# Lightning attention and a mixture of depths: the twelfth 128-token group as one wide chunk, and the expert's first pieces among the products of that step

## The chip, the cores and the metric

The kernel runs on one core of a Trainium2 chip. A core has five engines that run side by side, each with its own instruction queue: TensorE (PE; its weight loads are shown apart as PEld), VectorE (DVE), ScalarE (ACT), GpSimd (POOL) and SyncE (SP). SP only issues DMA transfers here, ACT and POOL issue some as well, and 16 DMA engines carry all of them. The time is the device time of one execution, in microseconds (us); less is better.

## The reference

There are two parts, all in float32. The first is a linear attention with decay, for 4 batches, 8 heads, 768 tokens and head size 64. In words, for each head with its decay `lam`:

```python
intra = (q_b @ k_b.T * Dmask) @ v_b          # Dmask[i,j] = lam**(i-j) for i >= j, else 0
inter = (q_b * lam**(pos+1)) @ kv_state      # what the earlier blocks left
out_b = intra + inter
kv_state = lam**block * kv_state + (k_b * lam**(block-1-pos)).T @ v_b
```

The reference cuts the tokens into blocks of 64. The result doesn't depend on the block length, apart from rounding, as long as the powers follow it.

The second part takes the attention's output `x`, the 8 heads side by side (512 values a token). A score `x @ w_gate` is made for each token. In each batch the 128 tokens with the highest scores go through an expert, and the others stay as they are:

```python
h = maximum(x[top] @ w1, 0)                  # 512 -> 1024
out[top] = x[top] + sigmoid(score[top]) * (h @ w2)   # 1024 -> 512
```

## The kernel before

**Groups and steps.** The 3072 tokens are 24 groups of 128 (`NG`), six to a batch (`NT`). Group `g` is rows `128*(g % 6)` of batch `g // 6`. One loop (L704) runs `g` from -1 to 23; one pass is called a step here. The order of all instructions is written out by hand (`manual_schedule`, L64), and each engine works through its own in that order. An instruction that waits therefore holds up everything behind it on its engine.

**Wide and narrow.** A group is either one chunk of 128 tokens ("wide") or two chunks of 64 ("narrow"). `wide(g)` at L192 decides by `WIDE`, which is 11: groups 0 to 10 are wide, 11 to 23 narrow. The batch ends lie at groups 5, 11, 17 and 23. The pieces of a group, each a function:

- `transposes(g, "qT" or "kT")` (L207): four TensorE transposes of the group's queries or keys into one PSUM bank, and an ACT copy to SBUF (L222).
- `queries_decayed(g)` (L224): POOL multiplies qT by powers of `lam` (L229 wide, L231 narrow) into `qs`. `keys_decayed(g)` (L195): the same for the keys, into `kd` (L200).
- `scores(g)` (L238): products of keys and queries into the PSUM tile `su`. Wide: 8 products of 64 by 128 (L249). Narrow: 16 of 64 by 64 (L255), into the first 256 columns of each half.
- `masked(g)` (L260): DVE multiplies the scores by the decay mask into `p`, 128x1024 when wide (L269), 128x512 when narrow (L275).
- `state_products(g)` (L281): `kd` times values. Wide: into a bank of its own (L293), and nothing for the last group of a batch, whose state nobody needs. Narrow: into the last 256 columns of `su` (L302); for the last group of a batch only the first chunk, since the second needs that state.
- `decay_state(n)` (L308, POOL L315) and `next_state(n)` (L320, DVE L332 and L334): the state of chunk `n` is the decayed old one plus the products.
- `from_states(g)` (L337: L344 wide, L355 narrow) and `from_scores(g)` (L363: L371 wide, L378 narrow): 16 products each into the PSUM tile `o`, the second on top of the first.
- `settle(g)` (L385): in narrow steps a small ACT copy that waits for the first of these sums. `outputs(g)` (L393): ACT copies `o` to `x_b`, one copy when wide (L400), three when narrow (L406, L408).
- `gate_scores(g)` (L418): DVE makes the tokens' scores, from `o` when wide (L422), from `x_b` when narrow (L429).

A float32 product shows as two matmul records and two weight-load records in the profile, so 16 products are "x32".

**Ranking and experts.** `row`, `compare`, `column_sums` (L439 to L493) count for each token how many tokens of its batch have a higher score; `find`, `tokens`, `fetch` pick the top 128 and gather their rows from the output in HBM. `expert(b, i)` (L546) returns 17 pieces for one batch: one `gate` (four transposes, L554, and an ACT copy, L559), eight `hidden` (L590, a Relu on ACT at L594) and eight `back` (L602). `products(n)` (L669) runs the next `n` of these pieces; its calls are strewn among the attention's products. `finish` (L610) runs at the next `flush()` after the last piece: a DVE operation (L615) and an indirect store on the POOL queue (L620).

**Banks.** Four PSUM banks `m` are handed out in turn by `bank()` (L176), the one used longest ago first. While an expert is in its `back` pieces one of them is held. A product into a bank waits until the last reader of that bank is done.

**A wide step** `g` (L714 to L802) does, in this order: the row and the comparison of group `g-1`, column sums, the transposes of group `g+1`, `queries_decayed(g+1)`, `from_scores(g)`, `outputs(g)`, `store(g)`, `gate_scores(g)`; then `state_products(g+1)`, `scores(g+1)`, `from_states(g+1)`, `keys_decayed(g+2)`, `next_state`, `decay_state`, and `masked(g+1)`. The last wide step, 10, differs because group 11 is narrow: it runs `scores(11)`, `masked(11)` and already the transposes of group 12 ahead of `state_products(11)`, and leaves `from_states(11)` to the next step.

**A narrow step** `g` (L803 to L850) does: `scores(g+1)`, `from_states(g)`, `settle(g)`, `load_v(g+2)`, `state_products(g+1)`, the first state, `masked(g+1)`, `from_scores(g)`, `outputs(g)`, `keys_decayed(g+2)`, a piece of the expert, column sums and the row of `g-1`, the transposes of `g+2`, the store, the second state, a `flush`, a piece, the comparison of `g-1`, `gate_scores(g)`, a piece, a `flush`. Where a batch ended six groups ago (steps 11 and 17) it begins with the expert's pieces and runs the first one ahead of all else (L804 to L807). So step 11 runs four pieces of batch 0's expert, and steps 12 to 15 three each.

**Loads.** SP issues keys and queries three groups ahead (L705), then parts of the expert's weights and the stores of batch 1; keys and queries have three buffers each, values six. The values of groups 2 to 13 are issued by ACT (`load_v`, L87): in wide steps from 4 on at the top of the step (L708), in narrow ones behind `settle` (L812).

Of the kernel before, what the change touches and what calls it, by code (L numbers as in the profile page):

```python
# [17 lines left out]
def kernel(  # L18
# [20 lines left out]
    NT = S // L  # L39
# [3 lines left out]
    NGR = (CAP + 127) // 128  # L43
    NG = B * NT
# [4 lines left out]
    SOON = 3  # L49
    SECOND = range(2, NT * 2 + 2)  # L50
    WEIGHTS = {9: 1, 10: 2, 11: 1, 12: 3, 13: 3, 14: 2}
    WIDE = 11
    FIRST_V = 4
    WARM = 8
    TINY = 2.0 ** -125
# [31 lines left out]
    def load_v(g):  # L87
        if g not in SECOND:
            return
        b, c = divmod(g, NT)  # L90
        nc.scalar.dma_start(
            out=loaded[g][2][:],
            in_=v[b, :, c * L : (c + 1) * L, :].rearrange("h p d -> p h d"),
        )
# [81 lines left out]
    def bank(hold=False):  # L176
        t = next(t for t in free if not any(t is x for x in held))
        free[:] = [x for x in free if x is not t] + [t]
        if hold:
            held.append(t)  # L180
        return t
# [5 lines left out]
    def quarters():  # L187
        for hp in range(NHP):
            for hh, c in ((0, 0), (1, 1), (1, 0), (0, 1)):
                yield hp, hh, c  # L190

    def wide(g):  # L192
        return g < WIDE

# [12 lines left out]
    def transposes(g, name, part=None):  # L207
        if g >= NG:
            return
        t = loaded[g][1 if name == "qT" else 0]  # L210
        dsts = qTs if name == "qT" else kTs
        hps = range(NHP) if part is None else range(part * NHP // 2, (part + 1) * NHP // 2)
        if not part:
            banks_[name] = bank()
            dsts[g] = att.tile([128, NHP, L], FP32, name=name)
        tp = banks_[name]
        for hp in hps:
            nc.tensor.transpose(  # L218
                tp[:, hp * L : (hp + 1) * L], in_=t[:, 2 * hp : 2 * hp + 2, :], identity=ident[:]
            )  # L220
        at = slice(hps[0] * L, (hps[-1] + 1) * L)
        nc.scalar.copy(out=dsts[g][:].rearrange("p a i -> p (a i)")[:, at], in_=tp[:, at])  # L222
# [15 lines left out]
    def scores(g, part=None):  # L238
        if g >= NG:
            return  # L240
        hps = range(NHP) if part is None else range(part * NHP // 2, (part + 1) * NHP // 2)
        qT, kT = qTs[g], kTs[g]
        if part != 0:
            qTs.pop(g), kTs.pop(g)
        if wide(g):
            to = o_ if part == 1 else su
            for hp in hps:
                for hh in range(2):
                    nc.tensor.matmul(  # L249
                        to[:, hh, hp * L : (hp + 1) * L], lhsT=kT[half[hh], hp, :],  # L250
                        rhs=qT[half[hh], hp, :], start=True, stop=True, skip_group_check=True,
                    )
            return
        for hp, hh, c in quarters():
            nc.tensor.matmul(  # L255
                su[half[c], hh, hp * C : (hp + 1) * C], lhsT=kT[half[hh], hp, half[c]],
                rhs=qT[half[hh], hp, half[c]], start=True, stop=True, skip_group_check=True,
            )

    def masked(g, part=None):  # L260
        if g >= NG:
            return
        if wide(g):
            if not part:
                ps_[g] = att.tile([128, 2, NHP * L], FP32, name="p", bufs=2)
            at = slice(0, NHP * L) if part is None else slice(
                part * NHP * L // 2, (part + 1) * NHP * L // 2
            )
            nc.vector.tensor_tensor(  # L269
                out=ps_[g][:, :, at], in0=(o_ if part == 1 else su)[:, :, at],  # L270
                in1=mask_w[:].rearrange("p a b i -> p a (b i)")[:, :, at], op=ALU.mult,
            )
            return
        p = att.tile([128, 2, NHP * L], FP32, name="p", bufs=2)
        nc.vector.tensor_tensor(  # L275
            out=p[:, :, : NHP * C], in0=su[:, :, : NHP * C],
            in1=mask[:].rearrange("p a b i -> p a (b i)"), op=ALU.mult,
        )
        ps_[g] = p

    def state_products(g):  # L281
        if g >= NG:
            return
        vn, kd = loaded[g][2], kds.pop(g)
        if wide(g):
            if g % NT == NT - 1:
                return
            ub = bank()
            us[g] = ub
            for hp in range(NHP):  # L290
                for hh in range(2):
                    h = 2 * hp + hh
                    nc.tensor.matmul(  # L293
                        ub[half[hh], hp * D : (hp + 1) * D], lhsT=kd[:, h, :], rhs=vn[:, h, :],
                        start=True, stop=True, skip_group_check=True,
                    )
            return
        for hp, hh, c in quarters():
            if c == 1 and g % NT == NT - 1:
                continue  # L300
            h = 2 * hp + hh
            nc.tensor.matmul(  # L302
                su[half[hh], c, NHP * C + hp * D : NHP * C + (hp + 1) * D],
                lhsT=kd[half[c], h, :], rhs=vn[half[c], h, :],
                start=True, stop=True, skip_group_check=True,
            )
# [202 lines left out]
    def tokens(b, i):  # L509
        e = hits_.pop((b, i))  # L510
        pk = bank()[:, :2]
        for t in range(NT):
            nc.tensor.matmul(
                pk, lhsT=e[:, t, :], rhs=place[:, b * NT + t, :],
                start=(t == 0), stop=(t == NT - 1),
            )
        two = mod.tile([128, 2], FP32, name="two")
        nc.vector.tensor_copy(two[:], pk)
        tok = const.tile([128, 1], I32, name=f"tok{b}_{i}")
        nc.vector.scalar_tensor_tensor(  # L520
            out=tok[:], in0=two[:, 0:1], scalar=128.0, in1=two[:, 1:2],
            op0=ALU.mult, op1=ALU.add,
        )
        toks[b, i] = tok
# [14 lines left out]
    def fetch(b, i):  # L539
        xs = mod.tile([128, HD], FP32, name="xs")  # L540
        nc.gpsimd.indirect_dma_start(
            out=xs[:], out_offset=None, in_=rows_upto(b), in_offset=rows_at(b, i),
        )
        xss[b, i] = xs
# [122 lines left out]
    pieces = []  # L667

    def products(n):  # L669
        for _ in range(min(n, len(pieces))):  # L670
            pieces.pop(0)()
# [15 lines left out]
    def ends(g):  # L687
        return g >= 0 and g % NT == NT - 1
# [15 lines left out]
    for g in range(-1, NG):  # L704
        loads_to(g + ahead(g), g)  # L705
        if g == 0:
            load_v(2)
        if FIRST_V <= g < WIDE:  # L708
            load_v(g + 2)
# [4 lines left out]
        if wide(g):  # L714
# [42 lines left out]
            if NGR and ends(g - 3):  # L757
                for i in range(NGR):
                    tokens((g - 3) // NT, i)
            if not wide(g + 1):  # L760
                scores(g + 1)
                masked(g + 1)
                for name in ("qT", "kT"):
                    transposes(g + 2, name)
            if g != 1:
                state_products(g + 1)
            if g > 0 and wide(g + 1):
                scores(g + 1)
            if wide(g + 1):
# [14 lines left out]
            if NGR and ends(g - 3):  # L784
                for i in range(NGR):
                    fetch((g - 3) // NT, i)
            if g > 1 and wide(g + 1):
                masked(g + 1)
            if g == 1:
                nc.scalar.copy(  # L790
# [10 lines left out]
                column_sums(g - 2)  # L801
                find((g - 2) // NT)  # L802
        else:  # L803
            if ends(g - 6) and g + 1 < NG:  # L804
                for i in range(NGR):
                    pieces.extend(expert((g - 6) // NT, i))
                products(1)  # L807
# [99 lines left out]
```

## Time and profile before

| | us |
|---|---|
| median of 3 runs (lowest, highest) | 173.01 (171.4, 173.9) |
| the profiled execution | 172.47 |
| its span, first to last instruction | 170.7 |
| PE busy | 160.3 (94%) |
| DVE busy | 107.0 (63%) |
| POOL busy | 86.8 (51%) |
| ACT busy | 71.0 (42%) |
| DMA: moved in the span | 32.20 MB |

The page's first part gives busy time and share of each engine. A second part cuts the span into 40 equal slices, one digit each, the busy share in tenths; PEclk is the clock granted to TensorE and DMA the mean share of the 16 DMA engines. The chain is the work that ended last, followed back from the last instruction: each step goes to what released it, or to the instruction before it on its engine. "issue" in it is time in which an engine waited for nothing that the profile shows. In a timeline a row is: start and duration in us, engine, line, operation, tiles written and read, shape, number of instructions, and in brackets how long the engine stood idle before and what ended that. Durations of single matmuls overlap, as TensorE is pipelined; the chain's pieces do not.

### The profile page before, as it was taken

The numbers are of one execution on the slowest core, as the hardware profiler recorded it, in microseconds if no ns is written. First come the engines' busy times: TensorE is split into PE (matmuls) and PEld (weight loads), VectorE is DVE, ScalarE is ACT, GpSimd is POOL, SyncE is SP. The second block draws the span as 40 slices with busy tenths as digits, with TensorE's granted clock in tenths as the row PEclk, the third lists the DMA queues.
The fourth block names the chain that finished last, engine by engine and source line by source line (L and its number), as shares of the span: only waits on it lengthen the run. The fifth ranks groups of instructions, "written<-read, shape, count | busy, mean of one in ns | idle before, by whom it ended". The sixth has DMA issues, their size and how long they took to land.

```text
span 170.7 us, 7463 instructions
## 1 busy us (share of the span) xinstructions
PE 160.3 (94%) x3228; PEld 134.1 (79%) x3228; DVE 107.0 (63%) x289; ACT 71.0 (42%) x188; POOL 86.8 (51%) x96
## 2 busy tenths in 40 slices
PE   7999999899899888999999999999999999999990
PEld 7788798788789767999767689998677698469970
DVE  1862569859986544685897996568879745340010
ACT  3355338434344344475346356635633553023100
POOL 1387864517759634485586659648767200201022
PEclk9999999999999999999999999999999999999998
DMA  4999999999999999999999988877024450111000
GB/s 107 223 222 214 238 198 268 279 276 296 236 262 277 284 314 218 349 213 317 256 220 205 246 211 177 187 217 217 28 103 139 161 198 3 20 45 61 0 31 31
DMA packets 82608, 32.20 MB, mean 189 GB/s; under 512 B 75792, under 2 KB 77840, under 8 KB 82576
## 3 DMA queue, kind: packets, MB, share of 16 engines
q1 hardware_dynamic: 66560, 21.50, 56.9%
q10 hardware_dynamic: 15360, 8.13, 18.6%
q0 software_dynamic: 656, 2.10, 3.8%
q8 instruction: 25, 0.41, 1.1%
q14 instruction: 7, 0.06, 0.1%
HBM read 24.38 MB, written 7.34 MB: 186 GB/s over the span
## 4 chain that ended last, share of the span: by engine, by line
PE 70%; DVE 7%; issue 6%; DMA 5%; POOL 5%; SPq 4%; ACT 1%; POOLq 1%; DVEq 0%
PE m L590 18%; PE m L602 13%; PE m L218 9%; PE su L255 4%; PE o L378 4%; PE o L371 4%; SPq L82 4%; DMA qn<-in_q_dram 4%; PE su L302 4%; PE su L249 3%; PE o L355 3%; POOL qs L229 2%; PE o L344 2%; PE m L449 2%; POOL kd L200 2%
## 5 line engine op out<-in xcount | busy, mean ns | idle before, releaser
L590 PE MATMUL m<-xsT,w_sb 128*128 128x128 f32 x256 | 32.3, 279 | 0.1
L590 PEld LDWEIGHTS m<-xsT,w_sb 128*128 128x128 f32 x256 | 29.9, 192 | 1.3 <-ACT xsT L559 0.8
L602 PE MATMUL m<-w_sb,hs 128*128 128x512 f32 (+1 forms) x80 | 30.9, 517 | 0.0
L315 POOL TENSOR_TENSOR decayed<-state,decay 128x256 f32<-128x256 f32 x21 | 16.7, 797 | 21.0 <-DVE state L334 13.5
L231 POOL TENSOR_TENSOR qs<-qT,qpow 128x512 f32<-128x512 f32 x13 | 17.9, 1376 | 2.6 <-ACT qT L222 2.6
L602 PEld LDWEIGHTS m<-w_sb,hs 128*128 128x128 f32 x80 | 13.9, 190 | 5.5 <-issue 4.3
L222 ACT COPY qT<-m 128x512 f32<-128x512 f32 (+1 forms) x25 | 14.2, 570 | 7.8 <-PE m L218 7.3
L222 ACT COPY kT<-m 128x512 f32<-128x512 f32 (+1 forms) x25 | 14.4, 574 | 5.8 <-PE m L218 5.8
L229 POOL TENSOR_TENSOR qs<-qT,qpow 128x512 f32<-128x512 f32 x9 | 11.5, 1273 | 10.0 <-ACT qT L222 9.9
L269 DVE TENSOR_TENSOR p<-su,mask_w 128x1024 f32<-128x1024 f32 (+1 forms) x11 | 12.9, 1170 | 5.7 <-PE su L249 5.7
L429 DVE CUSTOM_DVE_ANT_0 xg<-x_b,wg_b 128x512 f32<-128x512 f32 x15 | 15.5, 1031 | 0.0
L218 PE MATMUL m<-ident,qn 128*128 128x128 f32 x96 | 15.3, 281 | 0.1
L218 PE MATMUL m<-ident,kn 128*128 128x128 f32 x96 | 15.1, 279 | 0.3 <-DVE beat L461 0.2
L200 POOL TENSOR_TENSOR kd<-kn,kpow_w 128x512 f32<-128x512 f32 x11 | 11.4, 1044 | 6.4 <-DVE kpow_w L131 5.3
L594 ACT ACTIVATE hs<-m 128x128 f32<-128x128 f32 x32 | 8.8, 278 | 13.9 <-PE m L590 12.8
L334 DVE TENSOR_TENSOR state<-su,decayed 128x256 f32<-128x256 f32 x21 | 8.8, 420 | 8.7 <-PE su L302 8.2
L371 PE MATMUL o<-vn,p 128*64 128x64 f32 x352 | 13.2, 226 | 0.7 <-issue 0.6
L371 PEld LDWEIGHTS o<-vn,p 128*64 128x64 f32 x352 | 11.4, 138 | 2.9 <-issue 2.8
L200 POOL TENSOR_TENSOR kd<-kn,kpow 128x512 f32<-128x512 f32 x13 | 13.5, 1040 | 0.0
L452 ACT COPY sc_row<-m 128x128 f32<-128x128 f32 x24 | 6.2, 265 | 16.3 <-PE m L449 7.8
L475 DVE SCALAR_TENSOR_TENSOR ranks<-same,prev 128x1 f32<-128x1 f32 x20 | 12.2, 609 | 0.7
L249 PE MATMUL su<-qT,kT 64*128 64x128 f32 x168 | 12.3, 285 | 0.1
(88 smaller groups left out, 276.1 us busy)
## 6 DMA issues: line engine op xcount, KB each, us to landing
kn<-in_k_dram SPq DMA_DIRECT2D x23, 256.0 KB, 5.9
qn<-in_q_dram SPq DMA_DIRECT2D x23, 256.0 KB, 6.2
out_dram<-x_b ACTq DMA_DIRECT2D x18, 256.0 KB, 4.2
vn<-in_v_dram SPq DMA_DIRECT2D x12, 256.0 KB, 5.1
vn<-in_v_dram ACTq DMA_DIRECT2D x12, 256.0 KB, 5.0
w_sb<-in_moe_w_dram SPq DMA_DIRECT2D x4, 512.0 KB, 6.9
w_sb<-in_moe_w_dram SPq DMA_DIRECT2D x8, 256.0 KB
out_dram<-x_b SPq DMA_DIRECT2D x6, 256.0 KB
```

What stands on the lines that cost most here:

```text
L200: nc.gpsimd.tensor_tensor(out=kd[:], in0=loaded[g][0][:], in1=pw[:].rearrange("p a b -> p (a b)").unsqueeze(2).broadcast_to([128, H, D]), ...
L218: nc.tensor.transpose(tp[:, hp * L : (hp + 1) * L], in_=t[:, 2 * hp : 2 * hp + 2, :], identity=ident[:])
L222: nc.scalar.copy(out=dsts[g][:].rearrange("p a i -> p (a i)")[:, at], in_=tp[:, at])
L229: nc.gpsimd.tensor_tensor(out=qs[:], in0=qTs[g][:], in1=qpow[:], op=ALU.mult)
L231: nc.gpsimd.tensor_tensor(out=qs[:].rearrange("p a (c i) -> p a c i", c=2), in0=qTs[g][:].rearrange("p a (c i) -> p a c i", c=2), in1=qpow ...
L249: nc.tensor.matmul(to[:, hh, hp * L : (hp + 1) * L], lhsT=kT[half[hh], hp, :], rhs=qT[half[hh], hp, :], start=True, stop=True, skip_group_ ...
L269: nc.vector.tensor_tensor(out=ps_[g][:, :, at], in0=(o_ if part == 1 else su)[:, :, at], in1=mask_w[:].rearrange("p a b i -> p a (b i)")[: ...
L315: nc.gpsimd.tensor_tensor(out=t[:], in0=states[n][:], in1=(decay_w if wide(g) else decay)[:], op=ALU.mult)
L371: nc.tensor.matmul(o_[half[c], hh, hp * D : (hp + 1) * D], lhsT=p[:, hh, i0 : i0 + C], rhs=vn[:, 2 * hp + hh, :], start=(hp == 0 and g % N ...
L429: nc.vector.tensor_tensor_reduce(out=xg[:], in0=x_bs[b][:, t].rearrange("p a b e -> p (a b e)"), in1=wg_b[:], scale=1.0, scalar=0.0, op0=A ...
L590: nc.tensor.matmul(ph, lhsT=w1_sb[:, dc, f * 128 : (f + 1) * 128], rhs=keep["xsT"][:, dc, :], start=(dc == 0), stop=(dc == NDC - 1),)
L602: nc.tensor.matmul(py[:, e0:e1], lhsT=keep["hs"][:, f, :], rhs=w2_sb[:, f, e0:e1], start=(f == 0), stop=(f == NFC - 1),)
```

## The change

`WIDE` becomes 12, so group 11 is wide and the first narrow group is 12, the first of the third batch. Step 11 becomes the last wide step: it runs the wide order, with `load_v(13)` at its top and the transposes of group 12 inside it. In the branch for the step before the first narrow group (`not wide(g + 1)`) the order is new: the pieces of expert 0 are made there and the gate runs ahead of `scores(12)`; then come `state_products(12)`, a piece, the transposes of group 13 (now keys first), and another piece. `masked(12)` moves from right behind the scores to the place where wide steps have it, behind the state's update. Step 11 so runs three pieces where it ran four. The branch in narrow steps that starts an expert is kept from starting expert 0 a second time by `g > WIDE`; for step 17 it is as before.

```diff
-    WIDE = 11
+    WIDE = 12
...
             if not wide(g + 1):
+                for i in range(NGR):
+                    pieces.extend(expert((g - 6) // NT, i))
+                products(1)
                 scores(g + 1)
-                masked(g + 1)
-                for name in ("qT", "kT"):
-                    transposes(g + 2, name)
             if g != 1:
                 state_products(g + 1)
+            if not wide(g + 1):
+                products(1)
+                for name in ("kT", "qT"):
+                    transposes(g + 2, name)
+                products(1)
...
-            if g > 1 and wide(g + 1):
+            if g > 1:
                 masked(g + 1)
...
-            if ends(g - 6) and g + 1 < NG:
+            if ends(g - 6) and g > WIDE and g + 1 < NG:
```

## The prediction

> **What bounds the kernel now.** I read the page first: the engine shares, the 40 slices, the chain.
>
> ```profile
> PE 160.3 (94%) x3228; PEld 134.1 (79%) x3228; DVE 107.0 (63%) x289; ACT 71.0 (42%) x188; POOL 86.8 (51%) x96
> ...
> PEclk9999999999999999999999999999999999999998
> DMA  4999999999999999999999988877024450111000
> ...
> PE 70%; DVE 7%; issue 6%; DMA 5%; POOL 5%; SPq 4%; ACT 1%; POOLq 1%; DVEq 0%
> ```
>
> TensorE is busy 94% of the span at full clock and carries 70% of the chain. The DMA engines are saturated until about 100 us. So the question is what TensorE does and waits for where the change is made. The chain of waits, cut to 59.4 to 70.2 us (start, length, what), shows it: the end of step 10 and all of step 11.
>
> ```profile
> 59.46 0.62 PE su L255 x32
> 60.09 1.02 PE m L218 x8
> 61.11 0.41 issue
> 61.52 0.68 PE su L302 x16
> 62.20 0.59 PE m L554 x4
> 62.79 0.09 issue
> 62.88 0.70 PE su L255 x32
> 63.58 0.23 PE o L355 x16
> 63.81 0.93 issue
> 64.74 0.46 PE o L355 x16
> 65.20 0.47 PE su L302 x32
> 65.67 0.51 PE o L378 x31
> 66.18 1.09 PE m L590 x8
> ...
> 68.39 1.79 PE m L590 x16
> ```
>
> From 59.46, where from_scores(10) ends, to 70.18, where step 12 begins with scores(13), pass 10.72 us: 1.43 us without work (0.41, 0.09, 0.93) and four expert pieces (gate, L554; three hidden, L590).
>
> The two waits differ. At 61.11 TensorE stands before state_products(11); in VectorE's timeline masked(11) ends at 61.42. Both touch tile su, the mask reading its first 256 columns, the products writing its last 256, and the start follows the mask's end by 0.1 us. I take it that the products wait for the mask. At 63.81 the stop lies inside one run of 32 equal matmuls whose inputs were long made. The same sort of stop ("issue") lies at 46.56 and 58.66. Counting TensorE's matmul and weight-load records, these three stand at numbers 1731, 2243 and 2499: 512 and 256 apart. The instruction queue brings 25 packets and 0.41 MB, 16 KB each, for some 6,500 records. So I read them as instruction blocks that came late; of the four block edges in this stretch three cost 0.55, 0.57 and 0.93 us, the one at 52.17 nothing.
>
> **The change, part by part.** All sums are against the profiled execution (span 170.7, time 172.47 us), which lies 0.54 below the median of 173.01.
>
> *Group 11's matmuls.* Rows for the same kinds: wide scores are 16 instructions (L249) in 1.09 us, narrow ones 32 (L255) in 0.62: +0.47. Wide from_scores (L371) takes 1.08, narrow (L378) 0.51 to 0.56: +0.54. from_states is 0.65 either way (L344; here 0.23+0.46). state_products(11) goes, −0.68, because a wide last group returns early. Net +0.3 us of TensorE. The Trainium skill speaks against the change here: its page "TensorEngine Tiling (Array Packing)", Theoretical Speedup, gives up to twofold for a dimension of at most 64. Narrow products use four 64x64 tiles and the wide ones two, so by the rule the two replacements would cost 0.62+0.53 = 1.15 extra; by the rows they cost 1.01. I use the rows.
>
> *Other work of group 11.* next_state(22) on VectorE (0.42) and decay_state(22) on GpSimd (0.8) go. masked(11) grows from 0.68 to 1.22. On ScalarE settle (0.16) goes and one copy of 0.59 replaces 0.37+0.74. kd(11) is still made (1.04 on GpSimd), for nobody. I cost these at nothing. masked(11) follows gate_scores(10), which ends at 60.81, so it runs to 62.03; its reader from_scores(11) now comes behind transposes(12), at about 62.7. If that 0.7 us cover were gone, TensorE would wait for the mask.
>
> *New wait.* from_states(11) moves to the end of step 10 and overwrites o, which gate_scores(10) reads until 60.81. Wide scores(11) end at 59.46+1.09 = 60.55: TensorE waits 0.3 us, and row(10), transposes(12) and the rest of its queue behind it. Earlier wide steps cover this with state products; here there are none.
>
> *Step 11 rebuilt*, from 59.46: scores(11) 1.09; wait 0.30; from_states(11) 0.65; row and column sums 0.28 (51.79 to 52.05); transposes(12) 0.93; from_scores(11) 1.08; gate 0.68; scores(12) 0.65; state_products(12) 0.47; hidden 1.09; transposes(13) 0.91; hidden 0.90. Sum 9.03, so step 12 would begin at 68.5 instead of 70.18. One hidden fewer (0.90) is done by then. At equal work it is 9.03 against 9.82: −0.79 us.
>
> Do the inputs come in time? The gate's bank is that of row(10), which compare(10) frees at about 62.4; the gate comes at 63.8. xsT is copied by 65.2, its reader starts at 65.6. The mask is no longer queued ahead of state_products, so the 0.41 wait goes. kn(13) landed at 60.62 and qn(13), issued 0.4 us behind it, should be there well before 66.7. masked(12) now waits behind next_state(24), until about 66.7; scores(13) need su at 68.5.
>
> *Queues.* load_v(13) is issued by ScalarE at the top of step 11, about 60.1 instead of 65.28: the same 256 KB. transposes(12) move from step 10 to 11 and release kn(12), qn(12) some 2 us later, at 63; the loads reusing those buffers leave SP at 68.86 and 70.22, behind stores and weights. SP's order is unchanged. On GpSimd kd(13) passes ahead of decay_state(25): qs(12) to 64.2, kd(13) to 65.2, then the decay at 66.1 when its state exists. No wait. Before group 16, loads get tighter: its kn and qn landed at 82.11 and 83.97, used at 85.87; with TensorE 1.6 us earlier there are 0.3 us left.
>
> *The deferred piece.* The 17 pieces of expert 0 ended in step 16's first slot; now they end in its second (0.90; TensorE was busy 4.37 of 4.60 us there, so I charge all). Its finish moves behind compare(15) and gate_scores(16): VectorE's 0.74, the indirect store on GpSimd (1.03), and behind that qs(18), whose 1.27 us must end by step 18, some 4 us later. In return compare(15), whose bank the next gate waits for (0.23 us at 99.19), no longer queues behind that 0.74. I count −0.2, between 0 and −0.23.
>
> *Instruction blocks.* The edge at 64.74 moves into scores(12), at about 64.8. The 256 instructions before it now take 6.1 us, against 5.15 to the old stop, but vn(13) enters the saturated DMA queues ahead of that block. Bounds: 0 (the edge at 52.17) and 0.93 (the old one). I take 0.3, because the block arrived for 64.74 and would be asked for only a little later. The Trainium skill's page "Runtime: NRT & Kernel Launch", Instruction fetch mechanics, says crossing a block is mostly hidden: by it this term is 0 and the gain 1.0. The three stops contradict it wherever DMA is full. Later edges move by about 64 instructions; steps 12 to 16 show no such stop, so I take 0 there, with bounds 0 and about 2 (two or three stops of 0.57 to 0.93). A gain is excluded, as none is there to remove.
>
> *Sum:* −0.79 + 0.3 − 0.2 = −0.7 us: 171.8 profiled, 172.3 as a median. From step 17 to the end TensorE has one idle stretch above 0.15 us (0.30 at 136.49), so the difference should pass to the end.
>
> **The rivals.**
>
> *The piece is free* (chance 0.17). If step 16 has room for its second piece, because VectorE rather than TensorE sets its length (gate_scores took 3.50 us there, see below), and no block is late, the gain is 0.79+0.9+0.2 = 1.9 us: 171.1. Against it: the 4.37 busy of 4.60.
>
> *Late instruction blocks, slower than before* (0.25). Place: the edges in steps 12 to 15, where the DMA rows show 9s. The mechanism decides once 256 instructions pass in less than about 3.3 us. One edge there is as short now (74.89 to 78.16) and costs nothing, since slow hidden pieces follow the first edge; shifted, both ends lie in the fast attention products. Two or three stops of 0.57 to 0.93 are 1.1 to 2.8 us; less the gain of 0.7, about +1.2: 174.2.
>
> *VectorE held up at step 16 or 17, slower* (0.08).
>
> ```profile
> 93.70 3.50 DVE L429 CUSTOM_DVE_ANT_0 xg<-x_b,wg_b 128x512 f32<-128x512 f32 x1
> ```
>
> The usual 0.68 became 3.50 while GpSimd ran three operations without a break. If a shift puts such a hold before a bank or mask that TensorE needs, up to 2.8 us are lost, less 0.7: 175.1; with late blocks as well, 177.
>
> *As worked out* (0.50): 171.7 to 173.0.
>
> **How the numbers follow.** Likeliest is 172.3. The range takes in the free piece on one side and the late blocks on the other: 170.9 to 175.0. Two per cent is 3.5 us, about what a measurement of this kernel can tell from no change. The sums don't reach it downward: 0.03 for a gain I have missed. Upward only both slow rivals together or a lost load do: 0.07. Within: 0.90.
>
> **What would show it.** Right: no stop before state products in step 11; a stop of about 0.3 us before from_states(11), ended by VectorE's gate scores; step 12's first scores at 68.5 to 68.9; two back pieces in step 16; the last expert's gate about 0.7 us earlier than 150.6. Wrong: "issue" stops between 70 and 100 us, a TensorE wait for qn of group 16 near 84, a compare or mask late at step 17, or another end of step 11. The whole would be wrong if TensorE had hidden slack after step 16 that swallows 0.7 us, or if the medians differ by drift of the chip, the three runs of before being spread over 2.5 us.

## The result, and the profile after

The changed kernel is slower: 175.82 us median of 22 runs (173.51 to 185.1) against 173.9 (171.4 to 178.54), ratio 1.011, interval 1.007 to 1.016. Medians are over all executions; ratios and their intervals use only those within about 1.5% of the fastest of their kernel. I had forecast 172.3, against a median of 173.01 from three runs, which 22 runs moved to 173.9. The profiled execution took 175.66 us, span 173.9. Its page, the engine shares, two of the slice rows and the chain by engine:

```profile
PE 161.2 (93%) x3196; PEld 135.0 (78%) x3196; DVE 106.6 (61%) x288; ACT 70.5 (41%) x185; POOL 85.9 (49%) x95
...
PEclk9999999999999999999999999999999999999998
DMA  4999999999999999979999989795133360011000
...
PE 75%; DMA 10%; issue 4%; SPq 4%; DVE 3%; ACT 2%; POOLq 1%; ACTq 0%; DVEq 0%
```

The clock is the same, and TensorE's busy time rose by only 0.9 us while the span rose by 3.2. So TensorE waits more. The chain of the changed kernel, cut to the same stretch as before (start, length, what), shows that the loss is not there, where the change was made:

```profile
60.28 0.69 DVE xg L422
60.97 0.02 DVE sc L422
60.99 0.14 issue
61.13 0.69 PE o L344 x32
61.82 0.25 PE m L449
62.07 0.05 PE m L487 x3
62.13 0.93 PE m L218 x8
63.06 1.08 PE o L371 x32
64.14 0.58 PE m L554 x4
64.73 0.69 PE su L255 x28
...
65.95 1.09 PE m L590 x8
67.04 0.87 PE m L218 x8
67.91 0.89 PE m L590 x8
68.80 0.62 PE su L255 x32
```

From_scores(10) ends at 59.64 and step 12 begins at 68.80: 9.16 us where the prediction built 9.03 plus 0.3. The wait before the state products is gone, and the new one, before from_states(11) and ended by VectorE's gate scores, is there. The loss comes later. In TensorE's timeline after (start, duration, line, tiles, shape, number, and in brackets the idle time before):

```profile
82.96 0.56 PE L378 MATMUL o<-vn,p 64*64 64x64 f32 x21
85.78 0.45 PE L378 MATMUL o<-vn,p 64*64 64x64 f32 x11 [2.26 <-issue]
...
117.83 0.27 PE L487 MATMUL m<-ones,table 128*128 128x1 bf16 x5
118.88 0.27 PE L449 MATMUL m<-ident,sc 128*128 128x128 f32 x1 [0.79 <-DVE state L334]
```

The first stop lies in the middle of 32 equal products of step 14. In the count of all TensorE records (matmuls, weight loads and 74 semaphore and drain instructions) it is number 3523, the second 5058, and a small one of 0.15 us at 75.78 is 3011. All are 195 + 256 n, give or take one, like the three stops of the kernel before (1731, 2243, 2499); such a number is called an edge here, the 256 instructions between two a block, and a wait at it a block stop.

The whole difference by stretches, each bounded by the same matmuls in the two chains:

| stretch | before | after | difference |
|---|---|---|---|
| to the end of from_scores(10) | 59.46 | 59.64 | +0.18 |
| to the start of step 12 | 10.72 | 9.16 | −1.56 (of it −0.90 the piece that moved on) |
| to the gate of expert 1 | 29.01 | 32.53 | +3.52 (the piece 0.90, stops 2.41) |
| to the end | 71.5 | 72.6 | +1.1 (a stop of 0.79) |

Of +3.2 us, 3.20 are the three block stops, −0.66 is the gain at equal work, and 0.18 came before the change acts. About 0.5 us is left over: after the stop in step 14 the products restart (0.88 us for the 32 where 0.56 is usual), the state products of step 17, in which an edge lies, take 0.72 us where they took 0.47, and there are waits of 0.30 us at 110 and 0.26 at 153 us, partly matched by one of 0.30 us in the kernel before.

The gain at equal work hides something. It is counted against a stretch that held a block stop of 0.93 us. Without that stop the kernel before needs 10.72 − 0.93 − 0.90 = 8.89 us for the work that takes the changed kernel 9.16. In the profile of the lightened kernel before (below), where no stop fell into this stretch, it took 9.55 us, 8.65 without the piece. So the new order of step 11 is at least 0.27 us longer, and what it wins is the missing stop: the block that ends there takes 6.1 us instead of 5.15, and it came in time in every profile that has the changed kernel's order and edges up to that point.

### The profile page after: what moved, and what is told of

It is laid out like the page before. It is cut to its first block, busy times and chain, and to the rows that moved or that the text cites. A ratio compares the mean times of both kernels' runs of the same rounds, so it can differ in the third digit from the quotient of the medians.

```text
span 173.9 us, 7391 instructions
## 1 busy us (share of the span) xinstructions
PE 161.2 (93%) x3196; PEld 135.0 (78%) x3196; DVE 106.6 (61%) x288; ACT 70.5 (41%) x185; POOL 85.9 (49%) x95
## 4 chain that ended last, share of the span: by engine, by line
PE 75%; DMA 10%; issue 4%; SPq 4%; DVE 3%; ACT 2%; POOLq 1%; ACTq 0%; DVEq 0%
PE m L590 17%; PE m L602 12%; PE m L218 10%; PE o L371 6%; PE su L255 5%; PE o L378 4%; SPq L82 4%; PE su L249 4%; DMA qn<-in_q_dram 4%; PE su L302 3%; PE o L344 3%; PE o L355 3%; DMA vn<-in_v_dram 3%; PE m L449 3%; DMA xs<-out_dram,tok 2%
## 5 line engine op out<-in xcount | busy, mean ns | idle before, releaser
L315 POOL TENSOR_TENSOR decayed<-state,decay 128x256 f32<-128x256 f32 x20 | 16.0, 801 | 17.9 <-DVE state L334 16.9
L269 DVE TENSOR_TENSOR p<-su,mask_w 128x1024 f32<-128x1024 f32 (+1 forms) x12 | 14.1, 1175 | 5.7 <-PE su L249 5.7
L200 POOL TENSOR_TENSOR kd<-kn,kpow_w 128x512 f32<-128x512 f32 x12 | 12.5, 1044 | 6.6 <-DVE kpow_w L131 5.3
L371 PE MATMUL o<-vn,p 128*64 128x64 f32 x384 | 14.4, 225 | 0.5 <-issue 0.3
L371 PEld LDWEIGHTS o<-vn,p 128*64 128x64 f32 x384 | 12.5, 137 | 2.8 <-issue 2.5
L429 DVE CUSTOM_DVE_ANT_0 xg<-x_b,wg_b 128x512 f32<-128x512 f32 x14 | 14.5, 1036 | 0.0
L249 PE MATMUL su<-qT,kT 64*128 64x128 f32 x184 | 13.5, 285 | 0.1
L218 PEld LDWEIGHTS m<-ident,qn 128*128 128x128 f32 x96 | 10.9, 143 | 2.6 <-DMA qn<-in_q_dram 1.3
L200 POOL TENSOR_TENSOR kd<-kn,kpow 128x512 f32<-128x512 f32 x12 | 12.5, 1039 | 0.3 <-DMA kn<-in_k_dram 0.3
```

Source lines behind the costliest of these rows:

```text
L200: nc.gpsimd.tensor_tensor(out=kd[:], in0=loaded[g][0][:], in1=pw[:].rearrange("p a b -> p (a b)").unsqueeze(2).broadcast_to([128, H, D]), ...
L218: nc.tensor.transpose(tp[:, hp * L : (hp + 1) * L], in_=t[:, 2 * hp : 2 * hp + 2, :], identity=ident[:])
L249: nc.tensor.matmul(to[:, hh, hp * L : (hp + 1) * L], lhsT=kT[half[hh], hp, :], rhs=qT[half[hh], hp, :], start=True, stop=True, skip_group_ ...
L269: nc.vector.tensor_tensor(out=ps_[g][:, :, at], in0=(o_ if part == 1 else su)[:, :, at], in1=mask_w[:].rearrange("p a b i -> p a (b i)")[: ...
L315: nc.gpsimd.tensor_tensor(out=t[:], in0=states[n][:], in1=(decay_w if wide(g) else decay)[:], op=ALU.mult)
L371: nc.tensor.matmul(o_[half[c], hh, hp * D : (hp + 1) * D], lhsT=p[:, hh, i0 : i0 + C], rhs=vn[:, 2 * hp + hh, :], start=(hp == 0 and g % N ...
```

## The experiments

**My theory**, formed on these two profiles: TensorE's instructions arrive in blocks of 256. A block's packet (one transfer of 16 KB) is sent some time after the previous edge is passed, later when the DMA queues are full, and takes a further time until TensorE goes on. Where the 256 instructions pass faster than that, TensorE stops at the edge. The change moved the edges. **Rivals:** the added TensorE work, the deferred expert piece or the moved load of values costs the time; the stop near 118 us is a wait for VectorE, as its row says.

**The changed kernel again**, nothing edited.

> The changed kernel once more, nothing edited, for a second profile. Theory one (late instruction blocks, set by where the edges fall and by what else is queued on the DMA engines): the stops lie again at instruction numbers 195 + 256 n of TensorE, but how long each is varies from execution to execution; in all 2 to 5 us. Theory two (the work itself costs more): step 11 and the steps behind it are longer without such stops. Ratio 1.007 to 1.016 by both.

Ratio 1.018 (1.014 to 1.021). The stops were back at the same instruction numbers: 0.22 at 3011, 1.84 at 3523, 0.86 at 5058. (A stretch from 85 to 90 us at a granted clock of 0.70 adds to this execution's span.)

**The kernel before again**, nothing edited.

> The kernel before once more, nothing edited, for a second profile and as a measure of how far two timings of one kernel lie apart. Its block of TensorE instructions that ends near 78 us passes in 3.3 us; in the first profile it came in time because its packet was sent 0.7 us after the previous edge, in the lightened kernel before it was sent after 2.6 us and came 1.5 us late. If late blocks depend on the other transfers of the moment, this profile may show a stop there of 0 to 1.5 us, and none between 110 and 125 us, where no block passes in under 3.8 us. Ratio 0.995 to 1.005.

Median 175.1 (173.02 to 177.77, 4 runs) beside 174.11 (173.56 to 177.99, 7 runs) of the same kernel: four runs in a set are good to half a per cent or so. The block that ends near 78 us came in time again, its packet sent 0.21 us after the edge before. But a stop of 1.28 us stood at number 5059, where I had expected none: the kernel before isn't free of stops behind 100 us either. Behind 65 us the two profiles of the kernel before have block stops of 0 and 1.28 us in all, the two of the changed kernel 3.20 and 2.92.

**The load of group 13's values late again**, issued at 63.9 us; the changed kernel issues it at 59.7, the kernel before at 65.3.

```diff
-        if FIRST_V <= g < WIDE:
+        if FIRST_V <= g < WIDE - 1:
             load_v(g + 2)
...
                 outputs(g)
+                if g == WIDE - 1:
+                    load_v(g + 2)
```

> The changed kernel with the load of group 13's values issued by ScalarE behind outputs(11), at about 65 us, as late as in the kernel before, instead of at the top of step 11 (about 60 us). TensorE's instructions are the same. If that early load is what pushes SP's transfers back by 1.5 us from 66 us on and makes the block before 85 us late: the stop there shrinks below 1 us and the ratio falls to about 1.00 (0.992 to 1.005). If it is not: 1.007 to 1.016.

Ratio 1.0105 (1.007 to 1.014): no better. The stop at 3523 shrank to 0.19 us, but its neighbours took over, at numbers 3266 and 3779:

```profile
80.31 1.39 PE L590 MATMUL m<-xsT,w_sb 128*128 128x128 f32 x11 [0.84 <-issue]
83.87 0.45 PE L378 MATMUL o<-vn,p 64*64 64x64 f32 x11 [0.19 <-issue]
90.33 0.68 PE L378 MATMUL o<-vn,p 64*64 64x64 f32 x27 [0.50 <-issue]
```

So the early load isn't the cause of more than a small part. Behind 65 us this profile has 2.3 us of block stops, where the changed kernel's first two have 3.20 and 2.92.

**Four expert pieces in step 11 again.**

```diff
                     transposes(g + 2, name)
-                products(1)
+                products(2)
```

> The changed kernel with two expert pieces instead of one behind the transposes of step 11, so four in that step as in the kernel before; expert 0 ends in step 16's first slot again and its finish comes ahead of compare(15). If the deferred piece and the later finish cost time: 0.5 to 1 us less than the changed kernel, ratio 1.003 to 1.008, seen in steps 16 to 18. If the edges alone do: behind step 16 nothing changes, the stop near 118 us stays at 0.6 to 0.9 us; before it the edges lie 16 instructions earlier and the block ending near 84 us passes in about 3.3 us: ratio 1.007 to 1.016.

Ratio 1.011 (1.007 to 1.015), as without the edit. The deferred piece and the later finish are not the cause, as far as an interval of ±0.4% can tell. The stops stood at 3522 (1.14 us) and 5059 (2.06 us).

**Lighter DMA queues**, in both kernels; seven of the eight loads of the second weight matrix are left out, so the experts' outputs are not the reference's.

```diff
-    parts = [(w1_load, f) for f in range(0, NFC, 2)] + [(w2_load, f) for f in range(NFC)]
+    parts = [(w1_load, f) for f in range(0, NFC, 2)] + [(w2_load, 0)]
...
-                    py[:, e0:e1], lhsT=keep["hs"][:, f, :], rhs=w2_sb[:, f, e0:e1],
+                    py[:, e0:e1], lhsT=keep["hs"][:, f, :], rhs=w2_sb[:, 0, e0:e1],
```

> The kernel before with seven of the eight loads of the expert's second weight matrix left out (1.8 MB, steps 12 to 14); the back products all read its first part, so the experts' outputs are not those of the reference. Theory one: the DMA queues are less full from 65 to 85 us; the kernel before has no late block there anyway, so it gains little: ratio 0.990 to 1.000. Theory two: the same.

> The changed kernel with the same seven loads left out and the back products reading the first part (experts' outputs not the reference's); TensorE's instructions and block edges are those of the changed kernel. Theory one: with the DMA queues less full no block comes late between 65 and 90 us, the 2.26 us stop goes, and the kernel is faster than the lightened kernel before by the 0.7 us of the prediction: ratio to the full kernel before 0.985 to 0.997, below that of the lightened kernel before. Theory two (added TensorE work, the deferred piece): it stays 1.5 to 2 us above the lightened kernel before.

The lightened kernel before: 1.005 (1.002 to 1.009). The lightened changed kernel: 1.012 (1.007 to 1.018). The expectation that it would be the faster of the two failed: by these ratios it is 0.7% slower, where the full changed kernel is 1.1% slower than the full one before, and the intervals overlap. The profiles show why 1.8 MB less doesn't settle it. The lightened kernel before had late blocks of its own, one of them at the edge where the full one had been in time:

```profile
47.01 0.34 PE L344 MATMUL o<-state,qs 64*64 64x64 f32 x5 [1.17 <-issue]
59.93 0.80 PE L371 MATMUL o<-vn,p 128*64 128x64 f32 x18 [1.39 <-issue]
...
75.87 1.50 PE L590 MATMUL m<-xsT,w_sb 128*128 128x128 f32 x12 [0.74 <-issue]
80.86 0.45 PE L378 MATMUL o<-vn,p 64*64 64x64 f32 x12 [1.50 <-issue]
```

The lightened changed kernel had only 1.1 us of them behind 65 us in its profile, and there its span (171.8) is below the other's (173.3).

**The edges alone, in place.** In step 17, some products of scores(18) are done twice, which adds instructions and moves nothing else; the real scores overwrite them. 8 products are 32 instructions, 16 are 64.

```diff
             queries_decayed(g + 1)
+            if g == 17:
+                again(g + 1, 8)      # or 16: the first products of scores(18), once more
             scores(g + 1)
```

> The changed kernel with 8 of the 16 products of scores(18) done twice in step 17: 32 more TensorE instructions, 0.3 us, nothing before step 17 touched. Theory one (where the edges fall decides): the edges behind step 17 lie 32 instructions earlier in the program; the block that ended at 118.9 us and passed in 3.16 us now passes in 2.3 us and ends inside from_scores(20); the stop moves from the row's transpose into those products and lasts 0.5 to 1.6 us. Theory two (the stop belongs to the row's transpose, as the profile's releaser says, a wait for VectorE): it stays at the transpose, 0.6 to 0.9 us.

> The changed kernel with all 16 products of scores(18) done twice in step 17: 64 more TensorE instructions, 0.6 us, nothing before step 17 touched. Theory one: the block passes in 3.8 us and comes in time: no stop above 0.2 us between 112 and 125 us, so the kernel is not slower from the second expert's gate to the end (72.5 us) for 0.6 us of added work. Theory two: the stop of 0.6 to 0.9 us stays at the row's transpose, 73.3 us from that gate to the end.

This is the cleanest of the tests. With 32 more instructions (single time 178.16) the stop left the row's transpose for the products of from_scores(20), at number 5058 again. With 64 (175.06) it was gone. The timelines of TensorE, first with 32, then with 64 (their line numbers are 7 higher):

```profile
118.09 0.68 PE L385 MATMUL o<-vn,p 64*64 64x64 f32 x29
119.64 0.33 PE L385 MATMUL o<-vn,p 64*64 64x64 f32 x3 [0.87 <-issue]
```

```profile
116.72 1.16 PE L597 MATMUL m<-xsT,w_sb 128*128 128x128 f32 x8
117.71 0.27 PE L494 MATMUL m<-ones,table 128*128 128x1 bf16 x5
117.84 0.30 PE L456 MATMUL m<-ident,sc 128*128 128x128 f32 x1
```

In these executions the stop near 118 us so belongs to an instruction number and not to what is executed there. That its row named VectorE as the releaser in the changed kernel was a coincidence of time. But the time wasn't won: by the chain the run with 64 took 73.2 us from the second expert's gate to the end, 0.6 more than the changed kernel's 72.6, where 72.5 was expected. New waits of 0.15 and 0.39 us stand in step 17 itself, at from_states(17).

**The edges from step 11 on**: 24 products of scores(12) repeated, 96 instructions.

> The changed kernel with 24 products of scores(12) done once more in step 11: 96 more TensorE instructions, 0.9 us, nothing before step 11 touched. Theory one: no block between 65 and 135 us passes in under 3.9 us; the stops near 85 and 118 us shrink to 0.3 us or less, unless a packet is held for over 3 us; 0.9 us added, 1 to 3 us saved: ratio 0.998 to 1.010. Theory two (the changed order itself is slower): 0.9 us more than the changed kernel, ratio 1.016 or more.

Ratio 1.024, interval 1.002 to 1.046: too wide to decide. In its profile the stops near 85 and 118 us are gone. Others, at 3011 and 4291, took their place; TensorE's rows with a wait between 64 and 125 us are:

```profile
75.51 0.55 PE L218 MATMUL m<-ident,kn 128*128 128x128 f32 x3 [0.91 <-issue]
102.95 0.28 PE L255 MATMUL su<-qT,kT 64*64 64x64 f32 x4 [0.55 <-issue]
111.02 0.69 PE L385 MATMUL o<-vn,p 64*64 64x64 f32 x32 [0.30 <-ACT seen L398]
```

**The edges from the start**, by another warm-up: some full-size warm-up products are replaced by more, smaller ones of 64x64.

```diff
-    warm(WARM)
+    warm(5)
+    tiny(27)    # +96; +64: 6 and 18, or 3 and 21; +224: 2 and 62
```

> The changed kernel with 96 more TensorE instructions in its warm-up: five full-size warm-up products and 27 products of 64x64 in place of eight full-size ones, about the same time, before any data has landed. Every edge between two blocks of 256 TensorE instructions so falls 96 instructions earlier in the program. Theory one (the changed kernel is slower because the edges fall so that one block passes too fast and the next comes late, 2.26 us at 83.5 us and 0.79 at 118): counted on the profile after, no block between 60 and 135 us now passes in less than 3.9 us, so both stops should go, and the ratio to the kernel before should fall from 1.011 to about 0.994 (0.985 to 1.000). Theory two (the added TensorE work, the deferred piece or the moved transfers make it slower): the ratio stays at 1.007 to 1.016.

> The changed kernel with 64 more TensorE instructions in its warm-up (six full-size products and 18 of 64x64), as many as group 11 lost by becoming wide, so that from step 12 on the block edges lie nearly as in the kernel before. Theory one: the stop at 83.5 us goes; one block ending near 77 us passes in 2.6 us and may cost up to 1 us; ratio about 0.998 (0.990 to 1.005). Theory two: 1.007 to 1.016 as without the shift.

> The changed kernel with 64 more TensorE instructions in the warm-up, now three full-size products and 21 of 64x64, so that the warm-up ends earlier than the data arrives and the start isn't held up as in the first try (there the first row came 2 us late). Theory one (block edges): behind step 17 the edges lie as in the kernel before, the steady stop of 0.6 to 0.9 us near 118 us goes, and from the second expert's gate to the end pass 71.5 us (as in the kernel before and in the first try) instead of 72.4 to 72.8; ratio 0.998 to 1.008. Theory two (work): 72.6 us there, ratio 1.011 or more.

> The kernel before with 96 more TensorE instructions in its warm-up (five full-size products and 27 of 64x64). Theory one: blocks now pass in 2.3 us (ending near 66 us), 3.3 (near 102) and 3.5 (near 128), so one to three stops appear, 1 to 3 us in all; ratio to the unshifted kernel 1.005 to 1.02. Theory two: no difference, 0.997 to 1.003.

> The kernel before with 224 more TensorE instructions in its warm-up (two full-size products and 62 of 64x64). Theory one: blocks pass in 2.7 us (ending near 79 us) and 2.3 us (near 114): stops of 1 to 2 us at both, ratio to the unshifted kernel 1.01 to 1.02. Theory two: no difference, 0.997 to 1.005 (the warm-up may be some tenths longer).

| run | median us | before, same set | ratio to it (interval) |
|---|---|---|---|
| changed, +96 | 179.6 | 173.53 | none given |
| changed, +64 | 175.6 | 173.53 | 1.020 (1.014 to 1.027) |
| changed, +64, shorter warm-up | 178.96 | 174.11 | 1.024 (1.013 to 1.034) |
| before, +96 | 179.23 | 173.53 | 1.039 (1.030 to 1.049) |
| before, +224 | 174.29 | 173.53 | 1.004 (0.999 to 1.009) |

No shift helped the changed kernel, against the expectation. Two things are mixed in. The first row's transpose came at 24.4 to 27.3 us instead of 22.9, with waits for the first loads; the profiles of "+64, shorter" and "before, +96" also have a slice of low granted clock near 24 us. And in the full DMA stretch new edges were late: 1.42 and 1.21 us at 3011 and 3523 in the first row, 1.23 and 1.58 at 3266 and 3523 in the second, 1.81 at 3523 in the last. The stop near 118 us did go with +64 in both tries. My count of which blocks pass fast enough to be late was a poor guide here: in the first row the block that came 1.21 us late had passed in 5.8 us, its packet sent only 4.3 us after the edge before.

**The edges from step 4**: 40 or 24 products for group 5's scores done beforehand and overwritten, 160 or 96 instructions.

```diff
+            if g == 4:
+                again(g + 1, 40)     # or 24
             if g > 0 and wide(g + 1):
                 scores(g + 1)
```

> The changed kernel with 40 products of 64x64 for group 5's scores repeated in step 4, overwritten by the real scores: 160 more TensorE instructions, about 1.2 us. All block edges behind step 4 fall 160 instructions earlier in the program. Theory one: no block between 60 and 100 us passes in under 4 us; the stops near 85 and 118 us (1.2 and 0.75 us on average) go, and of the stops at 47 and 59 us some part: 1.2 us added, 2 to 3 saved: ratio 0.998 to 1.007. Theory two (the change's own order is slower): 1.2 us on top, ratio 1.016 or more.

> The changed kernel with 24 such products repeated in step 4: 96 more TensorE instructions, 0.7 us. Theory one: the block before 85 us passes in about 5.8 us, but a packet may be held for 3 to 4 us there, so a stop of up to 1.2 us may stay; none near 118 us; ratio 0.999 to 1.010. Theory two: ratio 1.014 or more.

Ratios 1.022 (1.014 to 1.030) and 1.015 (1.006 to 1.023), above what my theory gave. With 160 the stops near 47, 59, 85 and 118 us were gone from the profile, but one of 1.35 us at 33 us and this one, with its packet sent 5.6 us after the edge before, stood in their place:

```profile
64.37 0.69 PE L351 MATMUL o<-state,qs 64*64 64x64 f32 x19 [1.96 <-issue]
```

With 96, stops of 1.19 and 1.75 us stood at 3011 and 3523. No placing of the edges that I tried brought the changed kernel level with the kernel before.

**Another order**: the first piece of a narrow step ahead of from_scores, in both kernels.

```diff
             masked(g + 1)
+            products(1)
             from_scores(g)
             outputs(g)
             keys_decayed(g + 2)
-            products(1)
```

> The changed kernel with the first expert piece of a narrow step run ahead of from_scores instead of behind outputs, so that the 256 fast instructions of a step no longer lie in one stretch. Theory one: the shortest blocks get longer by up to 0.9 us, the stops near 85 and 118 us shrink; ratio 0.998 to 1.008, below the changed kernel's. If outputs coming 0.9 us later hold up the row and the comparison: 1.01 to 1.02.

> The kernel before with the same move of the first piece. Theory one: its blocks were seldom late behind 66 us, so little changes: ratio 0.993 to 1.005.

Both are slower than the kernel before: 1.027 (1.016 to 1.038) and 1.031 (1.021 to 1.040). The later outputs are one cost; in the changed kernel with this order TensorE waits for them near the end, and the kernel before with it has the same two waits:

```profile
141.98 0.69 PE L355 MATMUL o<-state,qs 64*64 64x64 f32 x32 [0.60 <-ACT x_b L408]
148.84 0.29 PE L449 MATMUL m<-ident,sc 128*128 128x128 f32 x1 [0.42 <-DVE ranks L491]
```

The block stops stayed (0.76 and 1.70 us in the one, up to 1.73 in the other), so this isn't a way round them.

**All profiles together.** In the 20 profiles TensorE stood idle for more than 0.45 us in 69 places behind 40 us. 62 of them are within 3 of an instruction number 195 + 256 n, whatever line stands there. The other seven have a transfer, ScalarE or VectorE as releaser. For the 85 stops at edges above 0.15 us behind 40 us, from the start of the block's packet to the restart passed 2.15 to 4.17 us, median 2.6. Most edges cost less than that: of the 217 between 40 and 100 us, 71 stopped TensorE for over 0.15 us.

How long after an edge the next packet is sent goes with the load of the DMA engines. Where they were busy for less than 20% of the first 0.7 us behind the edge (53 edges between 40 and 136 us) it was 0.86 us at the median and 2.4 at most; where they were busy for over 80% (253 edges), 2.43 and 5.6. That the packet waits behind the data is inferred from this; no view shows when it was asked for.

Whether the change would win without the stops can be read as well. From the last product of from_scores(10) to the end pass, block stops subtracted, 110.5, 110.7 and 110.6 us in the kernel before (first profile, again, lighter queues) and 111.3, 111.3 and 111.2 in the changed one (first, late load, lighter queues). That is 0.7 us more, not less. Restarts behind the stops are still in both, 0.32 us behind the longest, so how much of the 0.7 is the order of work stays open; a gain isn't there. (The second profile of the changed kernel is left out for its stretch of low clock.)

For the long stop of the changed kernel's profile, the DMA view of two windows, from the previous edge (80.14 us) to 83.0 and from 83.0 to 83.2, shows when its packet was sent (queue: packets, MB, share of 16 engines):

```profile
q1 hardware_dynamic: 1083, 0.89, 104.6%
...
q1 hardware_dynamic: 207, 0.05, 115.5%
q8 instruction: 1, 0.02, 31.9%
```

No instruction packet for 2.9 us while SP's queue filled all 16 engines; then one, 2.7 us before TensorE went on at 85.78. The 256 instructions had passed in 3.38 us: 2.92 + 2.71 − 3.38 = 2.25, the stop of 2.26. In the kernel before, the window from 75.5 to 75.7 us shows the same kind of packet for the block that had passed in 3.27 us:

```profile
q1 hardware_dynamic: 97, 0.03, 75.4%
q8 instruction: 1, 0.02, 34.2%
```

It was sent 0.7 us after the edge, and 0.7 + 2.6 is just 3.3: in time, by nothing.

## Why the prediction was wrong

*The rebuilt step 11* was right in its sizes. 9.16 us against 9.03 with 0.3 for a late block at 64.9, and that block came in time; the wait for the gate scores cost some 0.4 for 0.3, and from_states 0.69 for 0.65. At equal work the gain is 0.66 us where −0.79 + 0.3 was set. But the −0.79 was never a gain of the order: the 9.82 it starts from holds the stop of 0.93 us, and without it the sum is 8.89 against 9.03, a small loss. The Trainium skill's "TensorEngine Tiling (Array Packing)" (Theoretical Speedup), by which the two wide replacements would cost 1.15 us extra instead of the rows' 1.01, didn't matter at this size: from_scores(11) took 1.08 us, as in the rows.

*The deferred piece* took 0.86 us in step 16's second slot, and the gate of expert 1 no longer waited for the comparison (−0.23). As worked out; the run with four pieces was no faster.

*The step that failed* is "Later edges move by about 64 instructions; steps 12 to 16 show no such stop, so I take 0 there, with bounds 0 and about 2". It measured 0.15 + 2.26 + 0.79 = 3.20 us in the first profile and 2.92 in the second, beyond its upper bound. Three errors are in it. The absence of stops in one execution of the kernel before was taken for a property of the kernel; it was in time by nothing at 78 us, and another execution had 1.28 us at 115. So "none is there to remove" didn't hold either. The price of a stop was bounded by the three stops seen, 0.57 to 0.93, though nothing limits it to that: it is the packet's delay plus some 2.6 us less the block's duration. And the place was set at steps 12 to 16, where step 20 had one as well. (The instruction numbers named in the prediction count the semaphore instructions too; by matmuls and weight loads alone the three stops lie 504 and 251 apart.)

So the rival "late instruction blocks" is what happened. It had been given a chance of 0.25, and 174.2 us. Its point of decision, 256 instructions in less than about 3.3 us, doesn't hold: the two large stops had 3.38 and 3.16 us, but the three stops of the kernel before followed blocks of 5.1 to 5.8 us, and later runs had blocks of up to 6.5 us late, where the packet was sent 4 us and more after the edge. The rival of a VectorE hold did not come: gate_scores took 3.50 us in step 15 of the changed kernel too, and TensorE didn't wait for it. The Trainium skill's page "Runtime: NRT & Kernel Launch" (Instruction fetch mechanics), which has the crossing mostly hidden, fits two thirds of the edges between 40 and 100 us, where the DMA engines are full; the other third, 71 of 217, stopped TensorE, and every profile here has some of them.

The range ended at 175.0. The 0.8 us beyond it can be put down to the reference median, 173.01 from three runs, 173.9 from 22: 1.011 times the former is 174.9. The direction can't: −0.7 us was expected and +1.9 measured.

*What is shown and what isn't.* Shown: the stops belong to instruction numbers; added instructions move or remove them, in single profiles; the early load and the deferred piece are not the main cause; of the 3.2 us between the two profiled executions some 2.5 are block stops (4.52 us of them behind 40 us, against 2.05). The rest is there, with 0.5 to 0.8 us, in every pair of the profiles compared above, and the rival that the added TensorE work costs time isn't excluded for it: step 11 is 0.27 us longer or more at equal work. Not shown: a version with all blocks in time; none came out of the shifts. Which edge pays differs between executions, so how much of the 1.1% the stops cost on average stays open.

## What to carry to other kernels

Where TensorE runs thousands of small instructions and the DMA engines are full, add the fetch of its instructions to the sum: look for idle stretches without a releaser, count whether they lie 256 instructions apart, semaphore instructions included, and compare how fast each such block passes with how late its packet is sent. An edit that adds or drops some tens of instructions moves every later edge, and more than its own gain can be lost to that. Take such stops out of the stretch that you mean to rebuild before you count what the new order wins. Don't take a stop's absence in a single profile as a floor.

## What was not expected of the hardware

Under full DMA engines a block's packet was sent up to 5.6 us after the edge before, and at the late edges some 2.6 us more passed until TensorE went on. One such stop cost 2.26 us, more than the change had to win. Leaving out 1.8 MB of loads did not make these waits go away.
